# First expert's first 256 tokens in plain float32 instead of three-term float32r, and a scale moved into the instruction that takes the minimum

## The chip, the core and the metric

One core of one Trainium2 chip runs the whole program. The metric is device time in microseconds; the kernel before took 751.63 us (median of 3 runs, 747.41 to 753.83). TensorE multiplies matrices, VectorE (DVE), ScalarE (ACT) and GpSimd (POOL) work element by element, and the SyncE queue (SP) issues the loads. For most of its matrix products this kernel writes a float32 number as a high and a low float32r part and adds three float32r products.

## What is computed

Attention with a bias, then a mixture of four experts, then a gated layer. Cut to what matters:

```python
# 2 batches x 8 heads, 576 positions, head size 64 -> 1152 tokens of 512
scores = scale * q @ k.T + min(bias, 0), causal
x = softmax(scores) @ v                      # 1152 x 512
for e in range(4):                           # w1: 512 x 1024, w2: 1024 x 512
    out += p[:, e:e+1] * (relu(x @ w1[e]) @ w2[e])
result = (out @ w_a) * (out @ w_b) @ w_out
```

## The kernel before

Attention runs in four groups (`GROUPS`); group 0 is the first 256 tokens of the first batch, the others follow in an order of their own. Only group 0 multiplies plain float32: its queries and keys carry the bias in one more row, and its scores come out unscaled, so `st_softmax` multiplies the minimum by `SCALE` (line 631) and scales again in the exponential (line 632). For each pair of heads `st_av` writes the result as a high and a low part, `xh` and `xl`, through `split`: ACT copies the high part out of PSUM (line 75), DVE subtracts it for the low part (line 76).

While groups 1 to 3 of attention run, `beside` puts expert work between their steps, so that TensorE has something to do. Its stages are expert 0 on tokens 0 to 256, then expert 1 on tokens 0 to 256, 256 to 512 and 512 to 768. A stage's first layer is 8 units of 4 x 3 matmuls of 256 columns (`l1_unit`, `standing`), its second layer 2 units of 8 x 3 matmuls of 512 columns (`l2_unit`, `moving`); all go through `mm3`, which adds high x high, high x low and low x high. `advance` deals out attention steps by estimated expert time.

The weights come in pieces of 512 KB: a load on SP into one of three `raw` buffers (`load_piece`, line 151), then a split into `wh` and `wl` in `split_piece`: the first four pieces (`NFIRST = 4`) wholly on POOL (lines 216, 222), of the later ones the high part on ACT (line 220) and the low part by turns on POOL and DVE (line 222). An expert has 8 such pieces. SP issues its loads strictly in order; a load that waits for a free buffer holds all loads behind it. The buffers of q, k and v of group 1 to 3 (`qr`, `kr`, `vr`) are single, so the loads for the next head stand in the same queue. Of k, ACT writes a high part and POOL subtracts it (`ks`, lines 572 and 574); the scores need both.

The order in which each engine runs its instructions is made by a scheduler from the program's order and its own estimates. After attention comes the rest of the experts and the gated layer, which the change doesn't touch.

## Time and profile before

| | before |
|---|---|
| median of 3 runs | 751.63 us (747.41 to 753.83) |
| the profiled execution, whole | 750.41 us |
| its span in the trace | 748.7 us |
| TensorE (PE) busy | 711.3 us, 95% of the span |
| DVE / ACT / POOL busy | 532.7 / 335.3 / 413.4 us |
| TensorE idle in the first 121.87 us, with the 8.79 us before its first matmul | 25.8 us |
| TensorE idle in the remaining 627 us | 12.0 us |

The span is cut at 121.87 us because there the second head pair of group 2 begins, and from there on the engines' orders of the two kernels are almost the same. How to read it: a matmul's record is longer than the time it takes from its neighbours (matmuls overlap), so what one costs is the distance of starts in a row of equal ones.

### The profile page before, as it was taken

What the parts mean: (1) busy time and instruction counts of PE and PEld (TensorE: products, weight loads), DVE (VectorE), ACT (ScalarE), POOL (GpSimd) and SP (SyncE); (2) the same over time, 40 slices, a digit from 0 to 9 for tenths busy, and PEclk for the clock granted to TensorE, in tenths of its full rate; (3) what the DMA queues carried; (4) which work ended last, traced back from release to release, by engine and by line L of the source; (5) the groups of instructions that cost most, each with busy time, mean ns of one, the idle gap of its engine ahead of it and who ended that gap; (6) DMA issues with size and microseconds to landing.
All of it is one profiled execution on the core that took longest, in us unless ns stands there. A gap on an engine that the chain in (4) does not pass through costs nothing.

```text
span 748.7 us, 11078 instructions
## 1 busy us (share of the span) xinstructions
PE 711.3 (95%) x3868; PEld 624.1 (83%) x3868; DVE 532.7 (71%) x1119; ACT 335.3 (45%) x756; POOL 413.4 (55%) x330
## 2 busy tenths in 40 slices
PE   5878889999999999999999999999899999999997
PEld 3567778898889888888888888887788888888886
DVE  7777688785777786666555656779783888877764
ACT  4577779986723432223231234333545434242410
POOL 1796676765513653333330356587468688798600
PEclk9889999999999999999999999999999999999999
DMA  6465523453220211111110113223013232223003
GB/s 182 158 211 175 148 73 104 110 139 92 55 85 29 85 56 57 57 56 57 57 39 18 57 57 85 65 77 111 28 43 99 59 90 79 85 72 97 1 1 127
DMA packets 35096, 61.34 MB, mean 82 GB/s; under 512 B 3473, under 2 KB 19377, under 8 KB 35041
## 3 DMA queue, kind: packets, MB, share of 16 engines
q1 hardware_dynamic: 34864, 60.50, 26.9%
q8 instruction: 31, 0.51, 0.3%
q14 instruction: 25, 0.20, 0.1%
q10 hardware_dynamic: 176, 0.14, 0.1%
HBM read 55.02 MB, written 2.58 MB: 77 GB/s over the span
## 4 chain that ended last, share of the span: by engine, by line
PE 59%; DVE 15%; POOL 9%; ACT 6%; issue 6%; DMA 4%; SPq 0%; POOLq 0%; ACTq 0%; DVEq 0%
PE ps L264 29%; PE psq L264 20%; PE pst L264 4%; POOL wl L76 3%; PE av L692 2%; PE tr L655 2%; DMA kr<-in_kT 2%; PE sc L604 1%; ACT e L632 1%; POOL tp L157 1%; DMA raw<-in_w 1%; DVE tp L169 1%; DVE tp L165 1%; DVE h2l L76 1%; ACT wh L220 1%
## 5 line engine op out<-in xcount | busy, mean ns | idle before, releaser
L264 PE MATMUL ps<-wh,h2h 128*128 128x512 f32 x332 | 130.6, 393 | 0.0
L264 PE MATMUL ps<-wl,h2h 128*128 128x512 f32 x332 | 129.6, 390 | 0.0
L76 POOL TENSOR_TENSOR wl<-raw,wh 128x1024 fp32r<-128x1024 f32 x24 | 58.2, 2434 | 128.3 <-ACT wh L75 97.9
L264 PE MATMUL ps<-wh,h2l 128*128 128x512 f32 x332 | 125.8, 392 | 0.8 <-DVE h2l L76 0.8
L317 DVE SCALAR_TENSOR_TENSOR acc<-ps,pr,acc 128x512 f32<-128x512 f32 x111 | 82.3, 745 | 40.4 <-PE ps L264 39.8
L264 PE MATMUL psq<-xh,wh 128*128 128x448 f32 (+1 forms) x224 | 81.6, 364 | 0.1
L264 PE MATMUL psq<-xl,wh 128*128 128x448 f32 (+1 forms) x224 | 81.2, 363 | 0.0
L264 PE MATMUL psq<-xh,wl 128*128 128x448 f32 (+1 forms) x224 | 81.2, 363 | 0.0
L264 PEld LDWEIGHTS ps<-wh,h2l 128*128 128x128 f32 x332 | 62.1, 188 | 14.8 <-DVE h2l L76 1.7
L264 PEld LDWEIGHTS ps<-wh,h2h 128*128 128x128 f32 x332 | 62.4, 188 | 11.8 <-ACT h2h L75 0.2
L328 ACT ACTIVATE h2h<-psq 128x448 fp32r<-128x448 f32 (+1 forms) x56 | 29.6, 532 | 93.9 <-PE psq L264 73.5
L264 PEld LDWEIGHTS ps<-wl,h2h 128*128 128x128 f32 x332 | 62.4, 188 | 11.1
L76 POOL TENSOR_TENSOR wl<-sums,wh 128x1024 fp32r<-128x1024 f32 x24 | 58.2, 2423 | 4.9 <-ACT wh L75 4.8
L75 ACT ACTIVATE wh<-raw 128x1024 fp32r<-128x1024 f32 x24 | 25.5, 1062 | 67.8 <-PE ps L264 51.7
L655 PE MATMUL tr<-ident,e 128*128 128x128 f32 x240 | 45.2, 289 | 11.0 <-DVE el L673 6.4
L264 PE MATMUL psq<-tqh,wh 128*128 128x448 f32 x144 | 52.9, 368 | 2.1 <-DVE u L415 1.3
L264 PE MATMUL psq<-tql,wh 128*128 128x448 f32 x144 | 52.6, 365 | 0.0
L264 PE MATMUL psq<-tqh,wl 128*128 128x448 f32 x144 | 52.5, 364 | 0.0
L644 POOL TENSOR_SCALAR e<-e,r 128x448 f32<-128x448 f32 (+4 forms) x64 | 37.9, 596 | 25.1 <-DVE r L643 23.1
L157 POOL TENSOR_SCALAR tp<-tp 128x512 f32<-128x512 f32 x24 | 47.3, 1988 | 6.5 <-ACT tp L156 6.5
L673 DVE TENSOR_TENSOR el<-tr,eh 128x512 fp32r<-128x512 f32 (+5 forms) x80 | 38.5, 483 | 16.1 <-ACT eh L671 15.4
L415 DVE TENSOR_TENSOR u<-psq,s 128x448 f32<-128x448 f32 x48 | 29.6, 618 | 28.4 <-PE psq L264 22.3
(174 smaller groups left out, 1963.3 us busy)
## 6 DMA issues: line engine op xcount, KB each, us to landing
raw<-in_w SPq DMA_DIRECT2D x40, 512.0 KB
raw<-in_wa SPq DMA_DIRECT2D x12, 512.0 KB
raw<-in_wb SPq DMA_DIRECT2D x12, 512.0 KB
raw<-in_wo SPq DMA_DIRECT2D x12, 512.0 KB
kr<-in_kT SPq DMA_DIRECT2D x16, 288.0 KB
vr<-in_v SPq DMA_DIRECT2D x16, 160.0 KB
kb<-ks SPq DMA_DIRECT2D x16, 144.0 KB
out<-acc SPq DMA_DIRECT2D x9, 256.0 KB
```

What stands on the lines that cost most here:

```text
L75: nc.scalar.activation(out=hi, in_=src, func=AF.Copy)
L76: lo_eng.tensor_tensor(out=lo, in0=src, in1=hi.bitcast(F32), op=ALU.subtract)
L157: nc.gpsimd.tensor_scalar(out=t.bitcast(F32), in0=t.bitcast(F32), scalar1=2.0**-15, scalar2=GMAX, op0=ALU.max, op1=ALU.min,)
L165: nc.vector.scalar_tensor_tensor(out=t, in0=lo, scalar=29, in1=t, op0=ALU.logical_shift_right, op1=ALU.bitwise_or,)
L264: ins = nc.tensor.matmul(ps, lhsT=l, rhs=r, start=first and k == 0, stop=last and k == 2, skip_group_check=more)
L317: nc.vector.scalar_tensor_tensor(out=dst, in0=ps, scalar=share, in1=dst, op0=ALU.mult, op1=ALU.add)
L328: nc.scalar.activation(out=hh, in_=src, func=AF.Relu)
L415: nc.vector.tensor_tensor(out=out, in0=a, in1=b, op=ALU.add)
L644: (nc.gpsimd if j.gi else nc.vector).tensor_scalar(out=t.e, in0=t.e, scalar1=r, scalar2=1.0, op0=ALU.mult, op1=ALU.mult)
L655: ins = nc.tensor.transpose(ps[:, c - c0, :], t.e[:, k0 : k0 + P], ident)
L673: nc.vector.tensor_tensor(out=j.el[:, c0:c1, x], in0=src, in1=hi.bitcast(F32), op=ALU.subtract)
L692: ins = nc.tensor.matmul(ps[:, o:] if j.gi else ps[a : a + D, o:], lhsT=j.vs[:, c, :], rhs=e[:, c, o:], start=(m == 0), stop=(m == len(mms ...
```

## The change

Expert 0 on the first 256 tokens is no longer split. `st_av` copies the PSUM result of group 0 to a float32 tile `x32` (ACT) and splits that copy for the later experts (high on ACT, low on POOL instead of DVE). `load_w32` loads the plain weights of expert 0 straight to where TensorE reads them, in four steps of 2 x 512 KB; the second layer's two tiles take the same two places as the first layer's, so their loads wait until the units of the first layer that read those places are done. `plain_expert` does the two layers with one plain float32 matmul in the place of three float32r ones. The pieces that are split begin with expert 1, and `NFIRST` is 0, so none of them has its high part on POOL. The line-631 multiplication goes, since the minimum is now taken of scaled scores.

```diff
-NFIRST = 4
+NFIRST = 0
+W32_STEPS = (4, 7, 11, 15)
...
+    ckr = slab.tile([P, NC * SL], F32, tag="wh", name="ckr")
+    x32 = [ckr[:, o : o + NT0] for o in (3 * S, 0, NT0, 2 * NT0)]
+    w32 = {
+        (key, m): slab.tile([P, NC, SL], F32, tag=t, name="w32")
+        for key in ("w1", "w2") for m, t in enumerate(("wh", "wl"))
+    }
+    def load_w32(key, m):
+        src = {"w1": w1, "w2": w2}[key][m]
+        for two in (slice(0, 2), slice(2, 4)):
+            nc.sync.dma_start(out=w32[key, m][:, two, :], in_=src[:, two, :])
...
-                scale=-1.0,
+                scale=-1.0 if j.gi else -SCALE,
...
-        if j.gi == 0:
-            nc.vector.tensor_scalar(out=mn, in0=mn, scalar1=SCALE, scalar2=None, op0=ALU.mult)
...
             if j.h % 2:
-                split(xh[j.h // 2][:, x], xl[j.h // 2][:, x], ps, nc.vector)
+                c_ = j.h // 2
+                nc.scalar.activation(out=x32[c_], in_=ps, func=AF.Copy)
+                split(xh[c_][:, x], xl[c_][:, x], x32[c_], nc.gpsimd)
...
-    halves = [queue_expert(ex) for ex in range(2)]
-    stages = [(ex, halves[ex], *TURNS[0]) for ex in range(2)]
-    stages += [(1, halves[1], *turn) for turn in TURNS[1:-1]]
+    halves = {1: queue_expert(1)}
+    stages = [(1, halves[1], *turn) for turn in TURNS[:-1]]
...
+    def mm1(ps, w, x, start, stop):
+        ins = nc.tensor.matmul(ps, lhsT=w, rhs=x, start=start, stop=stop)
...
+        if mixed:
+            mixed[0](4 * (x.shape[-1] / 2400 + 0.013))
...
+    def plain_expert():
...
+        def first_(m, f):
+            ps = ps_m.tile([P, NT0], F32, tag="mm", name="ps1")
+            for c in range(NC):
+                mm1(ps, w32["w1", m][:, c, f * P : f * P + P], x32[c], c == 0, c == NC - 1)
...
+        def second(t):
+            ps = ps_m.tile([P, DM], F32, tag="mm", name="ps2")
+            for m in range(2):
+                for f in range(NF):
+                    mm1(ps, h32[m, f][:, t : t + P], w32["w2", m][:, f, :], m + f == 0, m == 1 and f == NF - 1)
+            add_share(ps, 0, t)
...
+        if state["n"] in W32_STEPS:
+            load_w32(*list(w32)[W32_STEPS.index(state["n"])])
...
-    beside = pipelined([expert_stage(*st) for st in stages], False)
+    beside = pipelined([plain_expert()] + [expert_stage(*st) for st in stages], False)
```

On SP, at the first loads of weights (`w_116`, `w_117` are the plain first-layer tiles, `kr_1_2` the keys of the second head of group 1) there stood before:

```order
L786 DMA pr<-in_dp 128x36
L151 DMA raw<-in_w 128x1024 x3
L557 DMA qr_0_2_389<-in_qT 128x384
L558 DMA kr_0_2_390<-in_kT 128x576
L559 DMA kb_0_2_391<-ckD 3x576
L559 DMA kb_1_2_444<-ckD 3x576
L581 DMA vr_0_2_464<-in_v 128x320
L151 DMA raw<-in_w 128x1024
```

and now stands, up to the loads of that head:

```order
L550 DMA w_116<-in_w 128x1024 x2
L153 DMA raw<-in_w 128x1024 x3
L571 DMA qr_0_2_390<-in_qT 128x384
L572 DMA kr_0_2_391<-in_kT 128x576
L573 DMA kb_0_2_392<-ckD 3x576
L573 DMA kb_1_2_443<-ckD 3x576
L595 DMA vr_0_2_462<-in_v 128x320
L550 DMA w_117<-in_w 128x1024 x2
L153 DMA raw<-in_w 128x1024 x2
L571 DMA qr_1_2_441<-in_qT 128x384
L587 DMA kb_0_2_392<-ks_0_2_434 64x576
L153 DMA raw<-in_w 128x1024
```

Four plain loads of 512 KB each have come in front of the keys of that head; the number of `raw` loads in front of them is 6 as before (three of them stand behind the rows shown before).

On ACT, at the end of group 0 (`av_6_0` is its last head pair, `ckr` holds `x32`), the copies that the first layer needs now stand so:

```order
L681 ACTIVATE eh_7_0_544<-tr_7_0_1_551 128x2x128
L586 ACTIVATE ks_1_2_493<-kr_1_2_442 128x576
L644 ACTIVATE e_0_2_2_536,l<-e_0_2_2_536,mn 128x320
L77 ACTIVATE vs_1_2_610<-vr_1_2_525 128x5x64
L644 ACTIVATE e_0_2_3_564,l<-e_0_2_3_564,mn 128x448
L652 ACTIVATE l<-l 128x1 x2
L717 ACTIVATE ckr<-av_6_0_541 128x256
L77 ACTIVATE xh<-ckr 128x256
```

Before, the copy of this head pair followed the last `eh` at once; now work on keys and values of the second head of group 1, which waits for their loads, and two exponentials stand between.

On PE, at the first units of expert 0 (`w_116` is the plain weight tile, `sc_1_2` the scores that need those keys), there now stands:

```order
L914 MATMUL ps_615<-ckr,w_116 128x256 x3
L702 MATMUL av_6_0_541<-eh_7_0_544,va 64x256
L702 MATMUL av_6_0_541<-eh_7_0_544,va 64x128
L620 MATMUL sc_0_2_4_554<-ks_0_2_434,qh_0_2_389 128x320
L621 MATMUL sc_0_2_4_554<-kb_0_2_392,qb_84 128x320
L620 MATMUL sc_0_2_4_557<-ks_0_2_434,qh_0_2_389 128x256
L621 MATMUL sc_0_2_4_557<-kb_0_2_392,qb_84 128x256
L914 MATMUL ps_641<-ckr,w_116 128x256 x3
L914 MATMUL ps_648<-ckr,w_116 128x256
L914 MATMUL ps_615<-ckr,w_116 128x256
L914 MATMUL ps_641<-ckr,w_116 128x256
L620 MATMUL sc_1_2_2_587<-ks_1_2_493,qh_1_2_440 128x320
```

Before, the first unit began only behind all of group 0 and stood whole; now 7 of the 32 matmuls of the first layer stand ahead of the first one that reads the last quarter of `x32` (the second row of `ps_615`), and 9 ahead of the scores of the second head.

## Rows read from the trace of the kernel before

**Rows 1.** The page's first part: busy time, share of span, instructions.

```profile
PE 711.3 (95%) x3868; PEld 624.1 (83%) x3868; DVE 532.7 (71%) x1119; ACT 335.3 (45%) x756; POOL 413.4 (55%) x330
```

**Rows 2.** Busy time by stretch; first line names the columns.

```profile
core 0: us, PE busy (x) PEld busy (x) DVE busy (x) ACT busy (x) POOL busy (x), PEclk, DMA share, GB/s
8.79:22.50 13.71, 13.68 (x41) 9.17 (x42) 10.33 (x63) 7.95 (x29) 5.10 (x11) 1.00 0.69 220
22.50:36.18 13.68, 11.44 (x48) 6.22 (x47) 10.63 (x44) 8.14 (x30) 10.62 (x9) 0.78 0.41 129
45.32:121.87 76.55, 64.45 (x440) 58.42 (x440) 58.50 (x165) 60.81 (x171) 54.90 (x59) 0.98 0.48 144
121.87:150.00 28.13, 27.69 (x183) 24.64 (x182) 21.30 (x88) 25.58 (x99) 18.88 (x33) 1.00 0.40 108
150.00:500.00 350.00, 348.51 (x1883) 311.02 (x1883) 235.03 (x444) 135.92 (x268) 157.81 (x104) 1.00 0.21 64
```

**Rows 3.** PE in order of time: start, duration, instruction, [idle before it <-releaser].

```profile
45.32 0.41 PE L606 MATMUL sc<-ks,qh 128*128 128x320 f32 x1 [2.60 <-POOL ks L574]
...
53.91 0.46 PE L655 MATMUL tr<-ident,e 128*128 128x128 f32 x1 [1.72 <-DVE el L673]
...
66.73 0.41 PE L607 MATMUL sc<-kb,qb 67*128 67x320 f32 x1 [1.32 <-DMA kb<-ks]
...
98.78 0.52 PE L655 MATMUL tr<-ident,e 128*128 128x128 f32 x3 [1.93 <-DVE el L673]
```

**Rows 4.** Weight splits between 45.32 and 121.87: busy us, mean ns, then idle.

```profile
L222 POOL TENSOR_TENSOR wl<-raw,wh 128x512 fp32r<-128x512 f32 x10 | 15.2, 1537 | 0.4 <-ACT wh L220 0.3
L222 DVE TENSOR_TENSOR wl<-raw,wh 128x512 fp32r<-128x512 f32 x10 | 12.8, 1320 | 4.2 <-ACT wh L220 4.2
L220 ACT ACTIVATE wh<-raw 128x1024 fp32r<-128x1024 f32 x10 | 10.3, 1052 | 3.1 <-DMA raw<-in_w 3.1
```

**Rows 5.** Chain that ended last, plain float32 matmuls: start, us, records.

```profile
24.83 0.43 PE sc L604 x2
25.27 0.79 PE av L692 x4
```

**Rows 6.** PE in order of time: float32r matmuls of 256 and 512 columns.

```profile
41.15 0.28 PE L264 MATMUL ps<-xh,wh 128*128 128x256 f32 x1
...
42.45 0.28 PE L264 MATMUL ps<-xh,wl 128*128 128x256 f32 x1
...
54.39 0.41 PE L264 MATMUL ps<-xl,wh 128*128 128x256 f32 x1
...
56.52 0.41 PE L264 MATMUL ps<-xh,wl 128*128 128x256 f32 x1
...
76.66 0.39 PE L264 MATMUL ps<-wh,hh 128*128 128x512 f32 x1
...
77.81 0.39 PE L264 MATMUL ps<-wh,hl 128*128 128x512 f32 x1
```

**Rows 7.** Chain that ended last: two loads from issue to landing.

```profile
34.82 4.99 DMA kr<-in_kT
...
98.11 3.87 DMA raw<-in_w
```

**Rows 8.** ACT in order of time around the second head's keys.

```profile
38.58 0.55 ACT L632 ACTIVATE e<-e,mn 128x320 f32<-128x320 f32 x1
...
39.83 0.68 ACT L572 ACTIVATE ks<-kr 128x576 fp32r<-128x576 f32 x1 [0.61 <-DMA kr<-in_kT]
...
41.62 0.36 ACT L296 ACTIVATE hh<-ps 128x256 fp32r<-128x256 f32 x1
```

**Rows 9.** POOL in order of time around the second head's keys.

```profile
37.70 5.90 POOL L222 TENSOR_TENSOR wl<-raw,wh 128x512 fp32r<-128x512 f32 x4 [4.41 <-ACT wh L220]
43.67 1.60 POOL L574 TENSOR_TENSOR ks<-kr,ks 64x576 fp32r<-64x576 f32 x1
```

**Rows 10.** The scaling of the minimum (line 631): ns min/median/max.

```profile
L631 DVE TENSOR_SCALAR mn<-mn x16: 133/146/154, 10.1 to 29.6; 128x1 f32<-128x1 f32 x16
```

More of the change, by code (lines that the diff above doesn't have):

```diff
@@ L534, in fused_kernel @@
     cum = vx[:NR, H * 2 * D :]
-    ckr = slab.tile([P, 3 * S], F32R, tag="wh", name="ckr")
-    ck3 = [ckr[:NR, j * S : j * S + S] for j in range(3)]
+    ckr = slab.tile([P, NC * SL], F32, tag="wh", name="ckr")
+    ck3 = [ckr[:NR, j * S : j * S + S].bitcast(F32R) for j in range(3)]
+    x32 = [ckr[:, o : o + NT0] for o in (3 * S, 0, NT0, 2 * NT0)]
[7 more added lines that the diff above has]
+            nc.sync.dma_start(out=w32[key, m][:, two, :], in_=src[:, two, :])
     def load_first(a, z, k_eng):
@@ L898, in pipelined @@
         return units + pend
+    def mm1(ps, w, x, start, stop):
+        ins = nc.tensor.matmul(ps, lhsT=w, rhs=x, start=start, stop=stop)
+        if len(passed) > LAG:
+            for name in passed[-1 - LAG]:
+                tc.add_manual_dep(ins.ins, name, NOSYNC, reason="the attention's pace")
+        if mixed:
+            mixed[0](4 * (x.shape[-1] / 2400 + 0.013))
+    def plain_expert():
+        h32 = {}
+        def first_(m, f):
+            ps = ps_m.tile([P, NT0], F32, tag="mm", name="ps1")
+            for c in range(NC):
+                mm1(ps, w32["w1", m][:, c, f * P : f * P + P], x32[c], c == 0, c == NC - 1)
+            h32[m, f] = h = pools["h"].tile([P, NT0], F32, tag="hh", name="h32")
+            if f % 2:
+                nc.vector.tensor_scalar(out=h, in0=ps, scalar1=0.0, scalar2=None, op0=ALU.max)
+            else:
+                nc.scalar.activation(out=h, in_=ps, func=AF.Relu)
+        def second(t):
[4 more added lines that the diff above has]
+            add_share(ps, 0, t)
+        T = 4 / 2400
+        l1 = [
+            (None, NC * (T * NT0 + 0.052), lambda m=m, f=f: first_(m, f)) for m in range(2) for f in range(NF)
+        ]
+        return l1, [(None, 2 * NF * (T * DM + 0.052), lambda t=t: second(t)) for t in range(0, NT0, P)]
     def expert_stage(ex, ws, t0, t1):
@@ L1083, in fused_kernel @@
     turn_t = [0.0]
-    for n in (2, 3, 4):
-        us = sum(c for st in stages[:n] for part in expert_stage(*st) for _, c, _ in part)
-        turn_t.append(us)
+    for n in (1, 2, 3):
+        parts = [*plain_expert(), *(part for st in stages[:n] for part in expert_stage(*st))]
+        turn_t.append(sum(c for part in parts for _, c, _ in part))
     SLACK = 15.0
```

4 lines of the change are left out of this document (1 added, 3 removed).

## The prediction

> **What bounds the kernel now.** I read the page's first part, then the busy time by stretch, then TensorE's instructions in order of time with the idle time before each. TensorE (PE) is busy 95% of the span, far ahead of the other engines [rows 1]. But the idle time is not spread evenly: from 150 to 500 us PE is busy 348.51 of 350 us, and between 121.87 and 150 still 27.69 of 28.13, while between 45.32 and 121.87 it is busy only 64.45 of 76.55 us [rows 2]. So there are two regimes. After 121.87 us the program costs what PE's instructions cost. The change doesn't touch them and the orders are the same there, so what it wins or loses before is handed on unchanged to the end. Before that, PE waits 12.1 us in one stretch and 2.24 us in the one of 22.50 to 36.18, and the waits have names: POOL's part of the keys (2.60 us), DVE's low part of the exponentials (1.72 and 1.93), a load (1.32) [rows 3]. DVE, ACT and POOL are each busy 72 to 79% of the stretch, and a part of that, 10 high parts on ACT and 20 low parts on POOL and DVE, is the splitting of weights [rows 4]. The change takes splits away there, and pays with PE time.
>
> **What PE pays.** A plain float32 matmul leaves two records. Two records of 256 columns take 0.43 us in the chain, so 0.215 each at full clock [rows 5]. A float32r matmul of 256 columns takes (42.45 - 41.15) / 11 = 0.118 us, one of 512 columns (77.81 - 76.66) / 5 = 0.230 us [rows 6]. Before, the first layer is 8 x 4 x 3 = 96 matmuls, 11.3 us, the second 2 x 8 x 3 = 48, 11.0 us: 22.3 us. After, the first layer is 32 plain matmuls, 64 records of 0.215 us, and the second 16 of 512 columns, 32 records. No row shows plain float32 with 512 columns; by the row of 256 doubled they take 0.43 each. Both layers are then 13.8 us. A record's 0.215 is twice 0.1075, so against the 0.118 of float32r it may lack some 0.01 us of cost between instructions; 96 records add 1.0. I take 28.5 us, **+6.2 us**. From below it is 27.5 us (+5.2). From above, the four records of a group-0 product with 256 and 128 columns took 0.79 us [rows 5] where 2 x 0.215 + 2 x 0.1075 = 0.645 were due; 0.036 more for each of 96 records makes 31.0 us (+8.7).
>
> **What the start gives.** Before, at 45.32 us PE has done 27 of the first layer's 96 matmuls and has just waited 2.60 us for the keys' low part [rows 3]. These were late because POOL first ran four weight splits for 5.90 us, up to 43.6 us, and only then 1.60 us for the keys [rows 9]. In the new order nothing of the weights stands on POOL ahead of them, so they follow the keys' load, which landed at 34.82 + 4.99 = 39.81 us [rows 7], by ACT's 0.68 and POOL's 1.60 us: ready at 42.1 instead of 45.3. A new wait takes that place: the copy of the last quarter of the expert's input stands on ACT behind those keys, two exponentials, the values and two sums. Before, ACT needed from 39.83 to 41.62 us for the same instructions but one exponential [rows 8]; with that (0.55) the copy starts at 42.2 and, taking 0.3 us (half a key copy of 576 columns), ends at 42.5. Until then PE can do the 7 matmuls ahead of it; two more of 2 x 0.225 us end at 43.4 with 9 of 32 done. That is the share 27 of 96, so the start gives 45.32 - 43.4 = **-1.9 us**. ACT's extra in the start (four high parts of 1.05 us and four copies of 0.3: 5.4 us) brings its stretch of 22.50 to 36.18 from 8.14 to 13.5 of 13.68 us [rows 2, 4]: full, so group 0's last product may come some 2 us later than 36.18, which the copy's 42.2 covers; without that cover each us would count. The 16 scalings of the minimum, 0.146 us each [rows 10], are 2.3 us of DVE. They lie beside PE, busy 13.68 of 13.71 us in the stretch before [rows 2]. I count nothing for them; at most they are worth the 2.24 us that PE idles up to 36.18. The same goes for the input's four low parts, now on POOL, and for the expert's hidden units, which need no low part any more: the plain matmuls wait for neither.
>
> **What the rest of the stretch gives.** Of the +6.2 us, 0.7 falls into the first 9 matmuls, which the start has counted; +5.5 is left. Against it stands idle time: 12.1 us, and 1.3 us in which PE ran at the lower of its two clock levels after a wait: from 54.39 to 56.52, 10 matmuls took 0.213 us each instead of 0.118, and two more the same [rows 6]. Of the 10 pieces split there before, 4 are split there in the new order: expert 1's other four come earlier, expert 0's not at all. That takes 6.3 us off ACT and 6 x 2 low parts, some 17 us, off POOL and DVE [rows 4]. If the waits go with the pieces, 4/10 of 13.4 us, 5.4, stay. The loads of the second layer's plain weights bring a wait of their own on SP: they wait for the first layer's units, and the next heads' keys stand behind them. 512 KB took 3.87 us alone [rows 7], two in a row some 6; beside them PE has a unit of expert 1 (12 x 0.118 = 1.4 us) and four plain matmuls of the half that has landed (4 x 0.88 = 3.5). I put the remaining 1.1 us for what sticks out and leave attention's steps there as a margin. So 13.4 becomes 6.5, **-6.9 us**. From below: as in the stretch of 121.87 to 150, where PE idles 1.6%: 1.2 us (-12.2). From above: all stays, and the SP wait is as long as its nearest row, 1.32 us, twice (+2.6).
>
> The sum is -1.9 + 5.5 - 6.9 = **-3.3 us** on the profiled execution's own 750.41, which is 1.2 us under the median of the runs; **747.0 us**.
>
> One rule speaks against this. PE waits about 1.5 us for the last quarter, a place where it didn't wait before. After the 1.72 us wait at 53.91 matmuls ran at half speed [rows 3, 6]; yet over the whole stretch, with all its waits, the granted clock was 0.98 [rows 2], which is 1.5 us lost in 76.55 and hardly more than that one place. So most waits cost no clock, and the sum leaves it out. The Trainium skill ("TensorE: Matmul & The Clock Gate", Part 1) says that the throttled clock is the default and that activity releases it, so a wait after sparse work would bring it back. By that rule the first matmuls behind this wait would run slowly as those at 54.39 did, +1.3 us, and the sum would be 748.3; the trace agrees at 53.91, not at the other waits.
>
> **The rivals.**
> - *The splits were nearly all of it.* Idle falls to the 1.6% of the next stretch: -1.9 + 5.5 - 12.2 = -8.6, 742 us. For it: POOL and DVE there are as busy as before, ACT even busier, and PE hardly waits [rows 2]. Against it: four pieces and the SP wait stay.
> - *The waits only change their cause.* The wait at 98.78 stands behind attention's own low parts, the one at 66.73 behind a load [rows 3]; if two thirds of 13.4 us stay and SP adds 2, 10.9 us of 13.4 stay, the stage gives -2.5 and the sum is +1.1: 751.5.
> - *The other side: the keys come late.* Ahead of the second head's keys SP now issues 4 x 512 KB more. If these 2.1 MB run in a row with the rest, at the 220 GB/s of 8.79 to 22.50 [rows 2] they take 9.5 us: the keys land at 49.3, the copy and PE behind them wait one for one, 747.0 + 9.5 = 756.5. Against it: DMA was busy only 41% from 22.50 to 36.18 us, 8.1 us free of 13.68, and at the full rate of 220 / 0.69 = 319 GB/s they need 6.6. It turns the gain into a loss once the keys land after 39.8 + 3.4 = 43.2 us.
>
> **How the numbers follow.** The forecast (744 to 750) has 0.47, the first rival (739 to 744) 0.20, the second (750 to 753.5) 0.20, the third (753.5 to 763) 0.13. About 1% is what a measurement can tell from no change here: 744.1 to 759.1 around the median. Faster by over 1%: the first rival and a little of the forecast, 0.22. Slower by over 1%: half of the third, 0.07. Within: 0.71. The range reaches into the first and the third rival until about 1 in 10 is left out on each side: 741 to 756.
>
> **What would show it.** In the new profile: two records of about 0.22 us per plain matmul of 256 columns, 0.44 of 512; one wait of PE near 41 to 42.5 us whose cause is ACT's copy; no POOL split ahead of the second head's keys; the group-2 scores that began at 121.87 now begin near 118.5; and, from there on, the same distance to the end. I am wrong in the price if those records are longer, in the start if the keys land past 43 us, in the stage if PE's idle time up to that score is not about half of 12.1 us, and altogether if the rest of the program doesn't carry the shift on unchanged.

## The result, and the profile after the change

The changed kernel takes 742.62 us (median of 4 runs, 742.23 to 744.09), beside 751.79 us for the kernel before in the same comparison: a ratio of 0.9883, with a 95% interval of 0.9844 to 0.9922. So 9.2 us are gone, a little over 1%. The forecast was 747.0 us, with a range of 741 to 756; the time lies in the range, near its lower end, and is almost exactly that of the first rival (742). The interval puts the gain between 5.9 and 11.7 us. The profiled execution took 742.59 us (span 740.9) against 750.41 us (span 748.7).

First the page's first part after the change, beside [rows 1]:

```profile
PE 716.4 (97%) x3820; PEld 622.9 (84%) x3820; DVE 523.8 (71%) x1091; ACT 331.1 (45%) x752; POOL 395.6 (53%) x318
```

Then the busy time by stretch of the same run, with the columns of [rows 2]. The bounds are moved to the same places in the program: 46.98 us is where 9 of the first layer's 32 plain matmuls are done (before: 27 of 96 at 45.32), and 115.33 us is the transpose that stood near 122 us before.

```profile
8.79:22.50 13.71, 13.63 (x41) 9.07 (x42) 9.20 (x54) 8.20 (x31) 1.69 (x8) 1.00 0.84 274
22.50:46.98 24.48, 22.67 (x74) 14.67 (x73) 15.52 (x47) 16.75 (x47) 14.94 (x14) 1.00 0.61 205
46.98:115.33 68.35, 65.75 (x406) 55.02 (x404) 52.66 (x158) 54.68 (x164) 43.79 (x51) 1.00 0.44 129
115.33:143.13 27.80, 27.46 (x185) 24.91 (x185) 21.75 (x92) 25.77 (x101) 19.46 (x33) 1.00 0.42 117
143.13:492.20 349.07, 347.43 (x1878) 310.27 (x1877) 234.12 (x439) 134.97 (x266) 156.65 (x102) 1.00 0.20 63
```

The reader is to see that PE now idles 2.6 us of 68.35 in the stretch in which it idled 12.1 of 76.55 [rows 2], and that the two stretches behind it look as they did. (The 1.00 in the first two rows is not the level of PE's clock there; the last section says why.) The waits of PE from 22 to 150 us, summed by cause (us in total, times, longest), are all that is left of [rows 3]:

```profile
PE tr L665 <- DVE el L683: 2.6, 4, 1.5
PE av L702 <- ACT eh L681: 1.2, 1, 1.2
PE sc L620 <- POOL ks L588: 0.6, 1, 0.6
PE av L702 <- DVE el L683: 0.2, 1, 0.2
```

**One ruler for all runs.** To compare kernels with different work in them, I take the stretch from PE's first score to one marker in the program: the 43rd product of a high key part (`sc<-ks`), of 80. Each kernel then has one row of the view by stretch, and its length is PE's busy time plus PE's idle time. Before, and after:

```profile
8.79:128.48 119.69, 102.46 (x613) 86.04 (x613) 91.00 (x307) 89.24 (x265) 81.78 (x89) 0.94 0.50 151
```

```profile
8.71:121.69 112.98, 108.16 (x564) 84.50 (x565) 82.12 (x279) 85.50 (x261) 64.09 (x77) 1.00 0.51 160
```

Busy 102.46 became 108.16 (+5.7), and idle 119.69 - 102.46 = 17.23 became 4.82 (-12.4): together -6.7 us. From the marker to the end of the span the kernels take 620.2 us and 619.2 us. So the gain is made in the first 120 us, as forecast, and the rest hands it on to within 1 us.

Why PE's busy time counts as a result too: it holds what the lower of the engine's two clock levels costs, since at that level a record takes twice as long (plain records of 256 columns start 0.427 us apart at 41 us in the changed kernel, 0.215 at 45 us). How long PE was busy at that level can be read off. A trace records each change of level, and ahead of the first one the products tell which it was: four value products (`av<-eh`) take 1.54 us at the lower level, 0.86 at the full one. Up to the marker PE was at the lower level in three stretches before, and in one after:

```profile
8.79:23.25 14.46, 14.43 (x44) 9.63 (x44) 10.62 (x65) 8.24 (x30) 5.85 (x11) 1.00 0.65 209
30.07:40.31 10.24, 9.68 (x36) 6.75 (x36) 7.21 (x17) 5.76 (x14) 5.74 (x5) 0.50 0.48 163
53.97:57.38 3.41, 3.41 (x16) 3.41 (x17) 2.55 (x4) 1.85 (x5) 3.33 (x3) 0.50 0.91 289
```

```profile
8.71:43.26 34.55, 32.65 (x95) 20.71 (x96) 23.15 (x94) 22.11 (x68) 13.09 (x17) 1.00 0.70 236
```

That is 14.43 + 9.68 + 3.41 = 27.5 us of busy time before and 32.7 after. Half of it is what the level costs, so of the +5.7 us 2.6 are clock and 3.1 the work itself.

### The profile page after: what moved, and what is told of

The parts are those of the page before. It is cut to its first block, busy times and chain, and to the rows that moved or that the text cites. A ratio compares the mean times of both kernels' runs of the same rounds, so it can differ in the third digit from the quotient of the medians.

```text
span 740.9 us, 10928 instructions
## 1 busy us (share of the span) xinstructions
PE 716.4 (97%) x3820; PEld 622.9 (84%) x3820; DVE 523.8 (71%) x1091; ACT 331.1 (45%) x752; POOL 395.6 (53%) x318
## 3 DMA queue, kind: packets, MB, share of 16 engines
q1 hardware_dynamic: 34864, 60.50, 25.4%
## 4 chain that ended last, share of the span: by engine, by line
PE 75%; DVE 11%; POOL 6%; issue 4%; ACT 3%; DMA 1%; POOLq 0%; ACTq 0%; DVEq 0%
PE ps L266 32%; PE psq L266 24%; PE pst L266 5%; PE av L702 4%; PE tr L665 3%; PE ps L914 3%; POOL wl L78 2%; PE sc L618 1%; PE sc L620 1%; PE sc L621 1%; POOL t L159 1%; POOL tp L159 1%; DVE t L171 1%; DVE el L683 1%; DVE tp L171 1%
## 5 line engine op out<-in xcount | busy, mean ns | idle before, releaser
L266 PEld LDWEIGHTS ps<-wh,h2h 128*128 128x128 f32 x332 | 62.4, 188 | 11.7 <-ACT h2h L77 0.2
L77 ACT ACTIVATE wh<-raw 128x1024 fp32r<-128x1024 f32 x24 | 25.5, 1062 | 67.5 <-PE ps L266 51.6
L644 ACT ACTIVATE e<-e,mn 128x128 f32<-128x128 f32 (+4 forms) x80 | 45.8, 572 | 10.1 <-DVE mn L631 9.7
```

The source lines that it names most:

```text
L77: nc.scalar.activation(out=hi, in_=src, func=AF.Copy)
L266: ins = nc.tensor.matmul(ps, lhsT=l, rhs=r, start=first and k == 0, stop=last and k == 2, skip_group_check=more)
L644: nc.scalar.activation(out=t.e, in_=t.e, func=AF.Exp, bias=mn, scale=-1.0, accum_out=t.l)
```

## The experiments

Theory A: what PE waited for were the splits of the first expert's weights; take them away and the waits go. Theory B: the plain matmuls' longer PE time covers attention's delays, and the splits are beside the point. In the forecast, the extra PE time and the idle time were two terms added up; under B they can't be.

**More PE time on the kernel before.** The splits stay, and the first expert gets a fourth term.

```diff
-        for k, (l, r) in enumerate(((lh, rh), (lh, rl), (ll, rh))):
+        pairs = ((lh, rh), (lh, rl), (ll, rl), (ll, rh)) if four else ((lh, rh), (lh, rl), (ll, rh))
+        for k, (l, r) in enumerate(pairs):
...
```

> The kernel before with the splits as they were, but the first expert's products get a fourth term (low part times low part): 32 more float32r matmuls of 256 columns (0.118 us) and 16 of 512 (0.230), 7.5 us more for PE and nothing for any other engine; nothing is left out. Theory A (what PE waits for is work of other engines that it can't outrun): all of it is paid, 753 + 7.5 = 760.5, 758 to 763. Theory B (a longer PE time covers the waits): PE is idle for 12 us in this stretch, so the longer work takes their place and hardly anything is paid: 751.5 to 755. In between, 755 to 758, both hold a part.

Measured: 754.22 us (10 runs, 749.72 to 755.43) beside 752.25, a ratio of 1.0016 [0.9990, 1.0042]. Of 7.5 us of new PE work 2 are paid (by the ratio's interval between none and 3.2). Its row up to the marker:

```profile
8.70:131.38 122.68, 112.03 (x661) 94.58 (x661) 88.03 (x307) 89.11 (x265) 80.71 (x89) 0.96 0.48 147
```

Idle is 10.65 us where it was 17.23: the longer work filled 6.6 us of waits. That is theory B's point, and it holds. What this trace is longer by (3.0 us) is clock: PE was busy at the lower level for 34.4 us instead of 27.5.

**The splits put back under the plain matmuls.** The weights are loaded in the old order again, and every piece gets its copy on ACT (or POOL) and two subtractions on POOL or DVE, on which the plain matmuls wait.

```diff
-        if state["n"] in W32_STEPS:
-            load_w32(*list(w32)[W32_STEPS.index(state["n"])])
+    for key, m in w32:
+        pieces.extend((("w32", key, m), "w32", False, {"w1": w1, "w2": w2}[key][m], j) for j in range(2))
...
-NFIRST = 0
+NFIRST = 4
...
+                    out=wl[:, m, :], in0=r[:, m - 2 * j, :],
+                    in1=zero[:].to_broadcast([P, SL]) if form == "w32" else wh[:, m, :].bitcast(F32),
```

> The changed kernel (plain float32 matmuls, PE's longer time) with the work of the splits put back where it stood before: the eight pieces of the first expert's weights are loaded in the old order, and each gets a copy on ACT (the first four pieces on POOL) and two subtractions of 512 columns on POOL or DVE, here of zero and in place, on which the plain matmuls wait. Nothing of the output is left out. Theory A: the waits come back on top of the plain price: 742.6 + 9 or more, 751 to 757 us. Theory B: the longer cover still hides them: 743 to 746 us.

Measured: 750.24 us (6 runs, 749.44 to 751.30) beside 753.12, ratio 0.9958 [0.9944, 0.9973]. Up to the marker:

```profile
8.66:128.44 119.78, 108.68 (x565) 84.75 (x566) 89.33 (x283) 88.67 (x265) 83.68 (x93) 0.96 0.48 151
```

PE's busy time is that of the changed kernel (108.68 beside 108.16); the idle time is 11.10 instead of 4.82. So the splits' work costs 6.3 us of idle time even under the longer PE work, nearly the whole 6.8 us by which this run's length exceeds the changed kernel's. Theory A's point holds as well, for about half of the 12.4 us with the longer PE work in place. (The run also puts the loads back into their old order, with the second expert's pieces behind the first's; the 6.3 us hold that too.) The time, 750.24, lies between the two forecasts, next to A's. And with the splits still there, the plain matmuls (and the change's other edits) are a little faster than the kernel before (0.9958), though PE has 5 us more to do.

**Only the low parts taken away, on the kernel before.** The three terms stay; the first expert's low parts aren't computed.

```diff
+            if form == "slab" and key[1] < 2:
+                slabs[key] = (slabs[key][0],) * 2
...
-            for m in (2 * j, 2 * j + 1):
+            for m in (2 * j, 2 * j + 1) if key[1] > 1 else ():
                 lo_eng.tensor_tensor(
```

> The kernel before, its three-term matmuls and their PE time unchanged, but the low parts of the first expert's weights are not computed (16 subtractions of 1.2 to 1.5 us on POOL and DVE); its matmuls take the high part in their place, so the low part's share is left out of the output. Theory A: the keys of the second head no longer stand behind POOL's splits (start -1.9 us) and most of the 12.1 us idle and 1.3 us of low clock go: 751.8 - 8 to - 12, 740 to 744 us. Theory B: attention's own delays stay and PE has no more cover than before: 748.5 to 752.

Measured: 748.34 us over four executions from 740.85 to 752.04, ratio 0.9898 [0.9843, 0.9953]; the profiled execution is the slowest of them, apart from the others, and not among those of the ratio. That is faster than before, but the interval reaches from 3.5 to 11.8 us of gain, where theory A asked for 8 to 12, and the median, 748.34, lies at the edge of theory B's range (748.5 to 752). Its trace has 14.3 us of idle time up to the marker (121.20 - 106.86), and three stretches at the lower clock level. How much of the splits' price lies in the low parts, and how much in the copies on ACT and in the loads that wait on SP for a free buffer, is not settled by it.

**What PE's time costs once the splits are gone.** In the changed kernel, 10 of the 48 plain matmuls (5.1 us) are left out, or done twice.

```diff
-                mm1(ps, w32["w1", m][:, c, f * P : f * P + P], x32[c], c == 0, c == NC - 1)
+                mm1(ps, w32["w1", m][:, c, f * P : f * P + P], x32[c], c == 0, c == NC - 1, c == 1)
...
-        ins = nc.tensor.matmul(ps, lhsT=w, rhs=x, start=start, stop=stop)
+        ins = None if skip else nc.tensor.matmul(ps, lhsT=w, rhs=x, start=start, stop=stop)
...
```

The second run has the same calls, and in their place:

```diff
+        if more:
+            nc.tensor.matmul(ps, lhsT=w, rhs=x, start=start, stop=False)
+            start = False
         ins = nc.tensor.matmul(ps, lhsT=w, rhs=x, start=start, stop=stop)
```

> The changed kernel with so many plain matmuls left out that TensorE has only as much to do for this expert as before: of the first layer one input quarter in four (8 matmuls, 16 records of 0.214 us), of the second layer 2 matmuls of 16 (4 records of 0.428 us), 5.1 us in all; part of the first expert's sum is so left out of the output. The splits stay away. Theory A: the stretch is bound by PE's instructions now (2.6 us idle in 68 us), so every us counts: 742.6 - 5.1 = 737.5, 736 to 739. Theory B: without the longer cover the waits come back, the idle time grows by about what is taken away: 741.5 to 743.5.

> The changed kernel with 10 plain matmuls of the first expert done twice (8 of the first layer, 2 of the second: 5.1 us of PE time at the full level; their share enters the output twice), the mirror of the run that left these 10 out and of the one that gave the kernel before a fourth term. There 7.5 us more on PE cost 2 us, since PE had waits that the longer work filled. The changed kernel has 2.6 us of waits left in 68, so nearly all should be paid: 743.4 + 5.1 = 748.5, 747 to 749.5. If other engines still set this stretch's length, 743.5 to 746.

Measured: left out, 742.00 us (4 runs, 741.28 to 742.48; ratio 0.9846 [0.9828, 0.9863]); done twice, 746.82 us (9 runs, 745.05 to 748.12; ratio 0.9937 [0.9911, 0.9964]). Their rows up to the marker, of the first and of the second:

```profile
8.73:119.09 110.36, 104.75 (x545) 80.60 (x546) 80.37 (x279) 84.45 (x261) 64.04 (x77) 1.00 0.53 163
```

```profile
8.74:125.90 117.16, 112.29 (x584) 87.61 (x585) 80.96 (x279) 85.22 (x261) 64.44 (x77) 0.97 0.49 154
```

Idle is 5.61 and 4.87 us, beside 4.82 in the changed kernel: with the splits gone, the waits neither come back when PE has less to do nor shrink when it has more. By the time alone the first run came out as theory B had it (741.5 to 743.5) and not as A (736 to 739); but what B gave as its reason, idle time that grows by what is taken away, is wrong in the trace. The second run missed its range (747 to 749.5) by 0.2 us. The first run also answers the main question: it has about as much PE work as the kernel before and no splits, and its idle time is 5.61 us instead of 17.23. So the splits' going, with the change's other edits, takes 11.6 of the 12.4 us without any longer PE work. The length moves by -2.6 and +4.2 us for -5.1 and +5.1 us of work, nearly all of it as busy time. In the second run the clock hides 1.9 us: PE was busy at the lower level for 28.9 us instead of 32.7. In the first it was 33.0, as in the changed kernel, and why only half of the 5.1 us shows there stays open. By the times, against the two sets of runs of the changed kernel (0.9883 here, 0.9900 below), taking the work away gains 0.6 to 4.1 us and doing it twice costs 2.8 to 4.2. So here more than half of added PE time is paid; on the kernel before it was 2 us of 7.5. That is how the larger of two needs behaves: with the splits there, the stretch up to the marker is about 120 us long with the shorter PE work (119.69) and with the longer (119.78); without them it follows PE's work (110.36, 112.98, 117.16).

**The changed kernel again,** as a base for the runs on the start:

> The changed kernel itself once more, beside the other runs of this call, as their common base: 742.6 us, 741.5 to 744. Its second trace shows whether PE ran the start (22 to 43 us) at the lower clock level by chance (then 1 to 3 us less in the start) or does so each time (same).

743.40 us (4 runs, 743.27 to 744.91), ratio 0.9900 [0.9884, 0.9915]. Its start runs as slowly as in the first trace (four value products in 1.54 us at 19.56, 23.58, 30.32, 33.90 and 37.83 us), and 5.43 us are idle up to the marker. So that is no accident of one execution.

**Fewer of the second expert's pieces in the start.**

```diff
-        if state["n"] > 3 and state["n"] % 2 == 0 and pieces:
+        if state["n"] > 3 and state["n"] % 4 == 0 and pieces:
```

> The changed kernel with half as many of the second expert's weight pieces loaded and split in the start (a step every fourth attention step instead of every second), so that fewer raw loads stand on SP ahead of the second head's keys and ACT, POOL and DVE have less to do there; the pieces come later, between 47 and 115 us. If the start is late for the reason the trace shows (keys issued at 37.21 us, landing at 42.08, behind raw loads that wait for splits), the ninth unit of plain work is done some 2 us sooner and the time is 740.5 to 741.5. If the splits moved into the stretch bring PE's waits back there, 744 to 748. If the start is bound by the lower clock level of PE up to 43 us, no change: 742 to 743.5.

Measured: 752.28 us (10 runs, 750.09 to 753.82), ratio 0.9999 [0.9972, 1.0026]: the whole gain is lost. None of my three cases says why; the trace does. In the changed kernel the last two plain weights are issued at 52.96 and 68.03 us. With fewer steps in between, the new order brings both forward into the start, right behind one another on SP. Its DMA issues (start, us, what):

```profile
30.16 1.78 SPq L550 DMA_DIRECT2D w<-in_w  x4
32.05 2.13 SPq L153 DMA_DIRECT2D raw<-in_w  x2
34.28 1.25 SPq L571 DMA_DIRECT2D qr<-in_qT  x1
...
37.79 0.33 SPq L572 DMA_DIRECT2D kr<-in_kT  x1
```

Six loads of 512 KB stand ahead of the second head's queries, which are issued at 34.28 and reach ACT at 43.51, 9.2 us later:

```profile
43.51 0.52 ACT L581 ACTIVATE qh<-qr 128x384 fp32r<-128x384 f32 x1 [2.92 <-DMA qr<-in_qT]
44.60 0.68 ACT L586 ACTIVATE ks<-kr 128x576 fp32r<-128x576 f32 x1 [0.57 <-DMA kr<-in_kT]
```

PE waits 3.30 us for a part of the first head's keys, and the second head's first score begins at 52.32 instead of 47.12 (in the second trace of the changed kernel):

```profile
43.96 0.98 PE L621 MATMUL sc<-kb,qb 67*128 67x320 f32 x2 [3.30 <-DMA kb<-ks]
```

That is the third rival of the forecast, the keys that come late, as it looks when it does happen. Not all of the loss is waiting: up to the marker PE idles 4.8 us more than in the changed kernel, and it is busy at the lower clock level for 40.0 us instead of 32.7, another 3.7 us. In the changed kernel the four pairs of plain loads stand apart (12.63, 19.87, 52.96 and 68.03 us), and the gain hangs on that.

**The input's low parts back on DVE.**

```diff
-                split(xh[c_][:, x], xl[c_][:, x], x32[c_], nc.gpsimd)
+                split(xh[c_][:, x], xl[c_][:, x], x32[c_], nc.vector)
```

> The changed kernel with the low parts of the expert's input computed on DVE, as before the change, instead of POOL (four subtractions of 256 columns, 0.72 to 1.17 us each on POOL). One of them, 0.77 us, stands on POOL right ahead of the first head's keys, behind which the second head's keys are loaded. If that queue is why the second head's keys come late (42.08 us), they come up to 0.8 us sooner: 742.6 to 743. If DVE, with its own splits there, is as full, the same or a loss of up to 1 us: 743 to 745.

743.69 us (4 runs, 743.03 to 744.32), ratio 0.9894 [0.9856, 0.9931]: no difference, as the forecast had it. It doesn't settle whether POOL's queue is why the keys come late: a weight split took the place on POOL, the first head's keys are done there at 36.58 instead of 36.77 us, and the second head's are issued only 0.2 us sooner (37.01 instead of 37.21).

**The scaling of the minimum, alone and undone.** First that part alone on the kernel before:

```diff
-                scale=-1.0,
+                scale=-1.0 if j.gi else -SCALE,
...
-        if j.gi == 0:
-            nc.vector.tensor_scalar(out=mn, in0=mn, scalar1=SCALE, scalar2=None, op0=ALU.mult)
```

> The kernel before with one part of the change alone: group 0's scores are scaled in the instruction that takes the minimum, and the 16 scalings of the minimum (0.146 us each, 2.3 us of DVE) are gone. Both theories of the gain (theory A: what PE waited for between 45 and 122 us were the splits of the first expert's weights; theory B: the longer PE time of the plain matmuls hides attention's own delays, and the splits are beside the point) expect nothing of it: 751.8 us, 749.5 to 753.5. If the scalings stood on the path of the start, it would be up to 2.2 us less, 749.5.

758.02 us (4 runs, 756.74 to 759.39), ratio 1.0060 [1.0036, 1.0083]: slower by 4.5 us with 16 instructions fewer, against both theories. Then the same part undone in the changed kernel:

> The changed kernel with that part undone: group 0's minima are scaled by 16 instructions of their own on DVE, as before (0.146 us each, 2.3 us). The order of all other work stays nearly the same. If the scalings lie beside PE's work: 742.6, 741.5 to 744. If they stand on the path of the start, where PE waited 2.24 us before: 744 to 745. The run of this part alone on the kernel before came out 4.5 us slower, with the whole order of the instructions shifted; if it is the instruction that costs and not the order, undoing it would gain: 738 to 740.

745.90 us (4 runs, 744.25 to 746.45), ratio 0.9925 [0.9904, 0.9945]: there it is worth about 2.5 us (1.9 by the ratios). The first f32r score begins at 37.89 us with the scalings, and at 36.83 and 36.90 without: 1 us of the start hung on them. So the instruction isn't the cost of the first run. What differs is the order: with the two traces' PE records laid side by side, 158 of 3868 are out of the common order in the first run, and 11 of 3820 where the part is undone in the changed kernel. The row of the first run up to the marker:

```profile
8.87:137.28 128.41, 109.11 (x612) 91.39 (x613) 90.58 (x291) 89.34 (x265) 81.06 (x89) 0.93 0.46 141
```

It is 8.7 us longer than before with the same matmuls: 2.1 us more idle, and 6.6 us more busy. Two of its waits and what follows the second one:

```profile
47.04 0.90 PE L652 MATMUL tr<-ident,e 128*128 128x128 f32 x3 [2.94 <-POOL e L641]
...
71.44 0.61 PE L607 MATMUL sc<-kb,qb 67*128 67x320 f32 x1 [2.97 <-DMA kb<-ks]
71.84 1.27 PE L652 MATMUL tr<-ident,e 128*128 128x128 f32 x5
72.76 0.56 PE L264 MATMUL ps<-xh,wh 128*128 128x256 f32 x1
73.12 0.42 PE L264 MATMUL ps<-xl,wh 128*128 128x256 f32 x1
73.34 0.41 PE L264 MATMUL ps<-xh,wl 128*128 128x256 f32 x1
```

The matmuls at 73.12 and 73.34 stand 0.22 us apart where 0.118 was due [rows 6]. Slice by slice the granted clock is 0.50 around 47 to 53, 71 to 77 and 115 to 118 us. Summed over these slices, the three places cost 3.4, 3.4 and 1.7 us, together 8.5; the kernel before has one such place (54 to 57.5 us, 1.7 us). The difference, 6.8, is the 6.6 us of busy time. (The two traces are 8.5 us apart, the medians 4.9, so these two executions show more of it than the average one.) Which of the moved instructions brought the waits about was not tried.

**PE given work before its first score.** PE stands still for the first 8.7 us. Here it multiplies zeros there, and in a second run with the same order ones in the form of the expert's own products.

```diff
+    warm = const.tile([P, P], F32, name="warm")
+    nc.gpsimd.memset(warm, 0.0)
+    wps = ps_m.tile([P, P], F32, tag="mm", name="wps")
+    for _ in range(14):
+        nc.tensor.matmul(wps, lhsT=warm, rhs=warm, start=True, stop=True)
```

> The changed kernel with 14 plain float32 matmuls of zeros (128 columns, two records each) on PE before its first scores, in the 8.7 us in which it waits for the first loads; their result is not used. In every trace of the changed kernel PE ran from its first score up to about 43 us at the lower clock level (four value products in 1.54 us; 0.86 at the full level). If the level of the start comes from PE having stood still before, the rows of the start take 0.86 us, the second head's scores begin sooner and the time is 738 to 741. If the level doesn't depend on that, or the start is bound by ACT, POOL and SP anyway, 742.5 to 744.5.

> The run with idle-time matmuls at the start once more, with the same order of all other instructions, but of ones instead of zeros and in the form of the expert's own products (8 plain float32 matmuls of 128x128 by 256 columns, 7 us at the lower level). With zeros the level did not rise: 28 records took 5.96 us, 0.213 each for 128 columns, and the start's value products 1.54 us; the run came out at 741.43 all the same. If the level rises with these, the start's rows take 0.86 us and the time is 737.5 to 740. If it doesn't, the time is that of the run with zeros, 740 to 743, and what that run gained over the changed kernel (about 1 to 2 us) came from the order of the start's work, not from the clock.

Measured: 741.43 us (4 runs, 739.40 to 742.69; ratio 0.9861 [0.9813, 0.9910]) and 740.76 us (6 runs, 739.67 to 742.35; ratio 0.9852 [0.9828, 0.9877]). Both are faster than the kernel before and the changed one, the second by 11.4 us over before and by 1.9 to 2.6 us over the changed one. The first lies between the two ranges given for it, the second in the one for a level that doesn't rise. The level did rise, though, in both. The row of the zeros as a whole, and its last three records:

```profile
1.05 5.96 PE L78 MATMUL wps<-warm 128*128 128x128 f32 x28 [1.05 <-POOL warm L75]
```

```profile
6.51 0.50 PE L78 MATMUL wps<-warm 128*128 128x128 f32 x3
```

The mean, 5.96 / 28 = 0.213 us, had me believe that all ran at the lower level; but the first record is longer than the rest, and the last three start 0.11 us apart instead of 0.213. The trace records the rise at 6.5 us. The first six score records behind them, and the same six in the changed kernel:

```profile
8.48 1.34 PE L624 MATMUL sc<-ka,qa 65*128 65x128 f32 x6 [1.47 <-DVE dif L791]
```

```profile
8.71 2.23 PE L618 MATMUL sc<-ka,qa 65*128 65x128 f32 x6 [8.71 <-DMA ka<-va]
```

From 10.33 us on four scores take 1.65 us again, and the stretch of 21 to 24 us is at the lower level:

```profile
21.00:24.00 3.00, 3.00 (x11) 2.10 (x9) 2.08 (x12) 2.46 (x9) 0.73 (x1) 0.50 0.99 342
```

With ones, PE's first rows are:

```profile
1.15 5.56 PE L78 MATMUL wps<-warm 128*128 128x256 f32 x16 [1.15 <-POOL warm L75]
...
10.61 0.92 PE L624 MATMUL sc<-ka,qa 65*128 65x256 f32 x4 [0.51 <-DVE mn L637]
...
12.27 1.65 PE L624 MATMUL sc<-ka,qa 65*128 65x256 f32 x4 [0.61 <-DVE mn L637]
...
15.77 1.54 PE L708 MATMUL av<-eh,va 128*64 128x256 f32 x4
```

Here the level rose on the way too (0.35 us for a record of 256 columns lies between 0.43 and 0.214), and four score records at 10.61 take 0.92 us; but from 12.27 on the same four take 1.65, and the value products 1.54 us. So the start's level was not raised for good in either, and the value products at 15.6 us begin hardly sooner than without (15.92). What these runs gain lies between 30 and 48 us: the second head's first score begins at 44.96 and 44.71 us instead of 46.98, and up to the marker PE is busy 105.63 and 105.41 us instead of 108.16. That is clock: PE was busy at the lower level for 26.6 and 25.4 us instead of 32.7, and half of the difference is 3.0 and 3.6 us. The level rose for good at 40.6 and 39.0 us instead of 43.3, and with zeros also for a while from 30.4 on. Whether the idle-time matmuls brought that about or the order of the work there (21 of PE's records moved) is not shown; in two runs without such matmuls (low parts on DVE, 10 matmuls more) the level also rose for a while from 32 us on.

**All runs on one ruler.** Up to the marker, in us, with the times; the second column is the part of PE's busy time at the lower clock level, read as above:

| kernel | PE busy | of it at the lower level | PE idle | length | median | ratio to before |
|---|---|---|---|---|---|---|
| before | 102.46 | 27.5 | 17.23 | 119.69 | 751.8 to 753.1 | 1 |
| changed | 108.16 | 32.7 | 4.82 | 112.98 | 742.62 | 0.9883 |
| changed, again | 108.47 | 32.8 | 5.43 | 113.90 | 743.40 | 0.9900 |
| before, four terms | 112.03 | 34.4 | 10.65 | 122.68 | 754.22 | 1.0016 |
| before, scale alone | 109.11 | 40.0 | 19.30 | 128.41 | 758.02 | 1.0060 |
| before, no low parts | 106.86 | 35.7 | 14.34 | 121.20 | 748.34 | 0.9898 |
| changed, splits back | 108.68 | 30.6 | 11.10 | 119.78 | 750.24 | 0.9958 |
| changed, 10 matmuls fewer | 104.75 | 33.0 | 5.61 | 110.36 | 742.00 | 0.9846 |
| changed, 10 matmuls more | 112.29 | 28.9 | 4.87 | 117.16 | 746.82 | 0.9937 |
| changed, fewer pieces early | 112.84 | 40.0 | 9.66 | 122.50 | 752.28 | 0.9999 |
| changed, scale apart | 108.64 | 32.8 | 5.61 | 114.25 | 745.90 | 0.9925 |
| changed, low parts on DVE | 107.41 | 30.0 | 5.39 | 112.80 | 743.69 | 0.9894 |
| changed, zeros ahead | 105.63 | 26.6 | 5.60 | 111.23 | 741.43 | 0.9861 |
| changed, ones ahead | 105.41 | 25.4 | 5.76 | 111.17 | 740.76 | 0.9852 |

Read down the idle column: about 17 to 19 us with the splits and three terms; about 11 with the splits and more PE work, whichever kind; about 5 without the splits, whatever PE has to do (9.7 where the loads stand in a row). Then take half of the second column off the first: 88.7 to 89.1 us in the three kernels with the PE work of the kernel before (before, scale alone, no low parts), 91.8 to 93.4 in the eight with that of the changed one. So where kernels with the same PE work differ in PE's busy time, by up to 7.4 us, it is the clock to within 1.6.

## Why the forecast was right in its direction and wrong in its parts

**The price of the plain matmuls** was taken as +6.2 us, between +5.2 and +8.7. Measured at the full level, eight records of 256 columns take 1.89 us and six of 512 take 2.74 us (these rows of the changed kernel):

```profile
52.34 1.89 PE L914 MATMUL ps<-ckr,w 128*128 128x256 f32 x8
...
76.44 2.74 PE L914 MATMUL ps<-w,h 128*128 128x512 f32 x6
```

Twelve of the first take 2.75 us at 44.58, so four more cost 0.86, 0.215 each, and 1.89 - 8 x 0.215 = 0.17 us is the last one's way to its end. With the same 0.17, a record of 512 columns is (2.74 - 0.17) / 6 = 0.428 us. The price is 64 x 0.215 + 32 x 0.428 - 22.3 = 5.2: the lower bound, without the cost between instructions that I had added. The term was right within 1 us. PE's busy time up to the marker can't confirm it: it grew by 5.7, of which 2.6 are clock, and why the other 3.1 are less than 5.2 was not followed up.

**The start** was forecast at -1.9 us and came out at +1.7: 9 of 32 done at 46.98 us instead of 43.4. The step that failed is PE's own time, which the forecast priced at the full level:

```profile
36.83 1.00 PE L620 MATMUL sc<-ks,qh 128*128 128x320 f32 x2 [0.61 <-POOL ks L588]
...
40.37 2.76 PE L914 MATMUL ps<-ckr,w 128*128 128x256 f32 x6
43.06 0.95 PE L702 MATMUL av<-eh,va 128*64 128x256 f32 x4
43.94 0.42 PE L620 MATMUL sc<-ks,qh 128*128 128x320 f32 x1
...
44.58 2.75 PE L914 MATMUL ps<-ckr,w 128*128 128x256 f32 x12
46.98 0.50 PE L620 MATMUL sc<-ks,qh 128*128 128x320 f32 x1
```

Six records take 2.76 us at 40.37 and twelve take 2.75 at 44.58: the lower level lasted up to 43 us. The stretch before, up to the same place, to be laid beside the second row of the changed kernel (22.50 to 46.98):

```profile
22.50:45.32 22.82, 17.99 (x83) 12.47 (x81) 17.12 (x59) 14.68 (x46) 18.11 (x14) 0.78 0.50 156
```

PE idles 1.8 us there instead of 4.8, so the waits went as hoped; but it is busy 22.67 us instead of 17.99. At the lower level it was busy for 19.0 us instead of 10.4 (from 30.07 to 40.31 and the first 0.7 us before; up to 43.26 after). Half of the difference, 4.3 us, is more than the 3.6 by which the step was off.

The keys were late as well, but that isn't what the start waited for. They were to land where they landed before, at 39.81 us; they landed at 42.08. SP tells why, and ACT what hung on it:

```profile
27.86 5.63 SPq L153 DMA_DIRECT2D raw<-in_w  x2
35.54 0.33 SPq L571 DMA_DIRECT2D qr<-in_qT  x1
...
37.21 0.39 SPq L572 DMA_DIRECT2D kr<-in_kT  x1
```

```profile
42.08 0.68 ACT L586 ACTIVATE ks<-kr 128x576 fp32r<-128x576 f32 x1 [1.73 <-DMA kr<-in_kT]
...
44.45 0.36 ACT L717 ACTIVATE ckr<-av 128x256 f32<-128x256 f32 x1
```

The second expert's raw weights hold SP from 27.86 to 33.5 us until splits free their buffers; then the single buffer of the queries comes free only when DVE has read it, at 35.51, and that of the keys when POOL has, at 36.77. So the keys are issued at 37.21 instead of 34.82 [rows 7], and the copy of the last input quarter is done at 44.8 instead of 42.5. I had followed ACT's and POOL's queues in the new order, but not that one on SP. Yet PE has no wait between 36.83 and 46.98: group 0's last product, which the copy reads, ends at 44.01 itself, and the copy is done 1.5 us ahead of the first matmul that reads it (46.31). The wait of 1.5 us for that copy, which the forecast had, isn't there. In the two runs with matmuls ahead the keys reach ACT almost as late (41.68 and 41.87 us), and the second head's scores begin 2.0 and 2.3 us sooner.

**The idle time** was forecast to go from 13.4 us (with 1.3 of clock) to 6.5, since 4 of 10 pieces would still be split there. Four pieces are indeed split there, by the changed kernel's trace; yet only 2.6 us of waits are left. The rule of proportion is the step that failed. Idle time isn't shared out by pieces; it is what the other engines need beyond what PE needs. With the splits gone that is little: 17.2 us of idle time become 5.6 at the PE work of the kernel before (10 matmuls fewer), so the splits suffice for 11.6 of the 12.4 us. With the splits there, PE's longer work would have covered 6 to 7 us of the same waits (four terms: 17.2 to 10.7; splits back: 11.1); the two don't add up. So the price was largely paid, as the sum had it, and the first rival named the right size (idle falls to a few us) and the right cause, though four pieces stayed. By the forecast's own sign (PE's idle time about half of 12.1 us) the stage was wrong.

**The sum.** The start came out 3.6 us worse than forecast, and the stretch behind it 6.8 better (68.35 - 76.55 = -8.2 us, where 5.5 - 6.9 = -1.4 were forecast). That the time lies in the range owes something to the two errors having opposite signs. (The terms add up to 747.1, not 747.0.)

**SP's own wait** for the second layer's weights (1.1 us put in the sum): the loads were issued at 52.96 and 68.03 us, and no wait of PE for a load is among the four causes listed above. The term is zero.

**The scalings** were counted as nothing, at most 2.24 us: they are worth 1 to 2.5, the bound. PE was busy 13.68 of 13.71 us beside them in the stretch that I had named as their cover, but the 2.24 us of waits behind that stretch were not covered; that the scalings stood on those is not shown.

**The rest** hands the shift on: right, within 1 us (620.2, 619.2, and 620.5 in the second trace of the changed kernel). **The third rival** was real, with another cause than the total of bytes: it came in full (+8.9 us over the changed kernel) as soon as the loads stood together, a good third of it as clock.

**The clock.** The forecast left it out but for one place, which it put at 1.3 us (its 12 matmuls, 0.095 us longer each, make 1.1; half of the 3.41 us of that stretch is 1.7). Up to the marker the level cost 13.8 us before and 16.3 after: 4.3 more in the start, 1.7 less behind it. In the nine traces that I went through, 28 waits of PE between 40 and 130 us are 1.2 us or longer, and 12 of them are followed by matmuls at the lower level, each such place costing 1.7 or 3.4 us; the changed kernel's one wait (1.52 us at 74.26, 1.82 at 75.20 in its second trace) is not: six records of 512 columns take 2.74 us right after. The 12 places cost 25.5 us, 0.9 for each of the 28 waits. So a wait that went took on average some 1 us of clock with it in these traces, and what decides which of them does isn't shown. No step of the sum had that, nor the longer start at the lower level.

## What to carry to other kernels

Where one engine is the bound in part of a stretch and waits in the rest, its extra work and its idle time are not two terms to add up: estimate the stretch from both sides, by what that engine needs and by what the others need, and take the longer. When work is moved to an earlier place, follow every load that is pulled forward with it on the queue that issues it, and what small load stands behind: 2 MB in a row ahead of one head's queries cost as much here as the whole change gained. Read the clock level of each stretch from the durations of like records before pricing it: here the level alone was worth as much as any term. And an edit of a few instructions can shift the order of more than a hundred: time a part alone and undone before giving it a price.

## What the runs showed of the hardware that was not expected

PE's start runs at the lower clock level however busy it is: 13.63 of 13.71 us busy up to 22.5 us, and four value products still take 1.54 us (0.86 at the full level) up to 38 us; matmuls in the idle time ahead of it raised the level, but only until 9.9 us (zeros) and 11.7 us (ones). The kernel before ran at the full level from 23 to 30 us in its one profiled execution, and in none of the traces of its variants, but then at the lower one until 40 us, where theirs rose by 36. Up to 45 us PE was busy at the lower level for 24.1 us in it and for 25.2 to 25.9 in them, so that trace flattered it by less than 1 us. The Trainium skill ("TensorE: Matmul & The Clock Gate", Part 1) has the throttled clock as the default, which activity releases. The traces agree as to the default, and show such a release at 43 us, after the expert's first products, and within the products of zeros (6.5 us) and of ones (4.9 us). But in the changed kernel PE was busy for 32.65 of the 34.55 us up to 43.26, and the level stayed low all that time.

The granted clock that the rows print is not to be trusted before the first change of level that a trace records. The changed kernel's row of 8.79 to 22.50 says 1.00 beside value products of 1.54 us; the run with zeros ahead says 0.50 beside the same 1.54. The column counts as full speed whatever lies ahead of the first recorded change. The changes themselves fit the durations where I compared them: 0.213 against 0.11 us at 6.5 us with zeros, 0.427 against 0.216 at 4.9 with ones, 1.54 against 0.86 at 23 in the kernel before. The same section of the Trainium skill warns that the recorded level changes on trn2 have been seen to be unreliable; no run here shows that. Durations of like records tell the level; the column alone does not.
